# Attention and token mixing on one core: the fourth pair of heads takes f32 weights turned on TensorE, and the fifth pair's scores move ahead of its products

## The chip, the cores and the metric

The kernel runs on one core of a Trainium2 chip. The metric is the device time of one execution in microseconds (us). The engines are named as in the profile: PE is TensorE (PEld its weight loads), DVE is VectorE, ACT is ScalarE, POOL is GpSimd, and SP is the queue from which all DMAs are issued. The granted clock of TensorE stands in the profile as a share of full speed: 1.00 is 2.4 GHz and 0.50 is 1.2 GHz.

## The reference

There are 8 batches, 8 heads, 576 positions and a head dimension of 64. Attention is masked to a window of 128 positions, with a bias that falls with distance; a token-mixing block follows on the concatenated heads.

```python
scores = scale * np.matmul(q, k.transpose(0, 1, 3, 2))
mask = (rel >= 0) & (rel < window)
scores = np.where(mask, scores + bias[None], -1000000000.0)
attn = np.exp(scores - np.max(scores, axis=-1, keepdims=True))
attn = attn / (np.sum(attn, axis=-1, keepdims=True) + 1e-09)
x = np.matmul(attn, v)                      # heads side by side: (8, 576, 512)
theta = x @ w_theta
zr, zi = x * np.cos(theta), x * np.sin(theta)
y = einsum('ts,bsd->btd', w_tok_r, zr) + einsum('ts,bsd->btd', w_tok_i, zi)
u = x + y
out = u + np.maximum(u @ w_ch, 0.0)
```

## The kernel before

The heads are worked in 32 pairs, p0 to p31; four pairs make one batch. For each pair, queries and keys arrive by DMA (`load_pair`), and are split into a high and a low part in fp32r (`split_high`: two ScalarE instructions, writing qh and kh; `split_low`: ql on VectorE, kl on GpSimd). Three products of these parts give the scores. Query positions are cut into five tiles; `SCORES` groups them as tile (0), tiles (1, 2) and tiles (3, 4). `weigh` (line 436) takes the scores from PSUM on VectorE, adds the band and finds the row's least value, and ScalarE applies the exponential (line 439). The weights of a pair lie in two halves in SBUF, called front and back.

Before the weights can multiply the values they must be turned. `flip(half)` does this in one of two ways. A pair with `early` set (the first `PLAIN` pairs) has eight f32 transposes of 128x128 on TensorE into PSUM and one ScalarE copy to pt (line 448); the products are then plain f32 (`ps<-vb,pt`). All other pairs get an f16 high and low half, hl (ScalarE line 453, VectorE line 455), which one DMA transpose turns into pt (line 457); values are split in the same way into vh and vl (lines 369 and 371), and three f16 products are summed. The scale for that split comes from the largest value of each head: a `measure` on VectorE, then `spread_from` and `spread_to`, which use a transpose of `peak` and a small matmul on TensorE.

`values` runs a pair's products over the five tiles and `finish` divides by the sums: denominator (line 486 or 488), reciprocal (491), x_sb (493), all on VectorE. When the four pairs of a batch are in x_sb, `turn` starts: x is transposed on TensorE into columns (L89, `ps<-fixed,x_sb`), split (x_hi at lines 532, 533 and 538; x_lo at 539), multiplied with w_theta (`mm<-wth_hi,x_hi`), and sine and cosine make z. `mix` multiplies z with w_tok, and `channels` makes the output.

The first batch is done by `start`, before anything else overlaps it. Its loop goes over pairs; in round p the pair p-1 has its first half turned, scores of pair p follow, then the second half, more scores, and the products of pair p-1. Between these it unpacks the w_theta and w_tok weights, which arrive as 64-bit floats, in many ScalarE and VectorE passes (lines 169 to 201). In the kernel before, the last round has no new pair: p3 is turned and multiplied alone, and p4's scores are issued after the loop. A scheduler orders the instructions of each engine by its own estimate of time in this part, so instructions of one pair can move ahead of another's; in the order of before, the first tile of p3's scores stands well ahead of the rest. From the first `mix` on, the order on TensorE is pinned to the program's.

PSUM has two rings here: `ps_s`, two tiles of two banks each, for scores of two tiles, turned weights, product sums and columns; and `ps_m`, four banks, for all others. A product sum can start only when the tile two uses earlier in `ps_s` has been read.

Of the kernel before, what the change touches and what calls it, by code (L numbers as in the profile page):

```python
# [20 lines left out]
B, H, S, D = 8, 8, 576, 64  # L21
# [9 lines left out]
DEPTH = 1  # L31
# [2 lines left out]
STEPS, FINISH = ((7, 7, 6, 3), (3, 4, 6, 4), (3, 4, 6, 3)), 250  # L34

GROUP = 4
PLAIN = 3
RINGS = ([("mx", 2 * NT, 4)] + [("den", 2 * NT, 3)] + [("whole", 1, 3), ("vs", GROUP, 3), ("scale", GROUP, 4)]
         + [("whole1", 1, 1), ("vs1", H, 1), ("scale1", H, 1)]
         + [("whole0", 1, 1), ("vs0", 9, 1), ("scale0", 9, 1), ("sum", 9, 1),  # L40
            ("row", 9, 1), ("inv", 9, 1), ("lim", 1, 1), ("t", 1, 2), ("zs", 9, 2), ("back", 1, 2)])
LOWS = float(np.float32(2.0 ** -29 * (1.0 - 2.0 ** -19)))
# [8 lines left out]
def attn_moe_kernel(ctx: ExitStack, tc: tile.TileContext, qt, kt, vx, wth, wtok, wch, band, out):  # L51
# [14 lines left out]
    uf = ctx.enter_context(tc.tile_pool(name="uf", bufs=2))  # L66
    big = ctx.enter_context(tc.tile_pool(name="big", bufs=1))
# [42 lines left out]
    peaks = [const.tile([128, 128], F32, name=f"peak{k}") for k in range(2)]  # L110
# [39 lines left out]
    def unpack(jobs, places):  # L150
# [65 lines left out]
        for k in range(n + 3):  # L216
# [12 lines left out]
    JOBS = ([(wth, wth_hi, wth_lo, c, DM, TURN) for c in range(4)]  # L229
            + [(wtok, wtk_hi, wtk_lo, c, S, "row") for c in ORDER])  # L230
# [18 lines left out]
    group_v = {}  # L249
# [7 lines left out]
    def measure(g, heads):  # L257

        nc.vector.tensor_reduce(out=peaks[g % 2][:, heads], in_=group_v[g][:, heads, :, :64],
                                axis=mybir.AxisListType.XY, op=ALU.max, apply_absolute_value=True)  # L260

    def spread(peak, n, part):
        return spread_to(spread_from(peak, n, part), n, part)
# [28 lines left out]
    def spread_first(g):  # L292
        peak = peaks[g % 2]
        nc.vector.tensor_scalar(out=peak[:, :GROUP], in0=peak[:, :GROUP], scalar1=2.0 ** -100, scalar2=None,
                                op0=ALU.max)
        group_v[g] = group_v[g], spread_from(peak, GROUP, "")

    def spread_scales(g):
        vb, diag = group_v[g]
        scale = spread_to(diag, GROUP, "")  # L300
        group_v[g] = vb, scale
        if g % 2:
            c = rings["scale"].at + (g // 2 - 1) % 2 * 2 * GROUP
            batch_scale(g // 2, fixed[:, c:c + 2 * GROUP])

    whole_w, first_scale = [], []

    def measure_first(g):
        nc.vector.tensor_reduce(out=peaks[0][:, GROUP * g:GROUP * g + GROUP], in_=group_v[g][:, :, :, :64],
                                axis=mybir.AxisListType.XY, op=ALU.max, apply_absolute_value=True)  # L310

    def clamp_first():
        nc.vector.tensor_scalar(out=peaks[0][:, :H], in0=peaks[0][:, :H], scalar1=2.0 ** -100, scalar2=None,
                                op0=ALU.max)
# [14 lines left out]
    def split_pair(p, raw):  # L329
        return split_low(split_high(p, raw))  # L330
# [21 lines left out]
    def split_values(n):  # L352

        k = n % GROUP
        if n < H:
            if k == 0:
                group_v[n // GROUP] = load_plain(n // GROUP)
            vb = group_v[n // GROUP]
            if n < 2 * PLAIN:
                return (vb[:, k],), None, None  # L360
            both = first_scale[0][:, n - n % 2:n - n % 2 + 2]
        else:
            vb, scale = group_v[n // GROUP]
            both = scale[:, k - k % 2:k - k % 2 + 2]
        vs = both[:, n % 2:n % 2 + 1]
        v = vb[:, k, :, :64]
        vh = vp.tile([128, 5, 65], F16, name="vh")
        vl = vp.tile([128, 5, 64], F16, name="vl")
        nc.scalar.activation(vh[:, :, :64], v, AF.Copy, scale=vs)
        nc.gpsimd.memset(vh[:, :, 64:], 1.0)  # L370
        low = nc.vector.scalar_tensor_tensor(out=vl, in0=v, scalar=vs, in1=vh[:, :, :64], op0=ALU.mult,  # L371
                                             op1=ALU.subtract)
        return (vh, vl), both, low
# [7 lines left out]
    SCORES = ((0,), (1, 2), (3, 4))  # L381
# [4 lines left out]
    class Pair:  # L386


        def __init__(self, p):
            self.p = p  # L390
            self.terms = parts.pop(p)
            self.early = p < PLAIN
            self.heads = [Head(2 * p + e, self) for e in range(2)]
# [279 lines left out]
    def prepare(p):  # L673

        if 0 <= p - 1 < pairs and p - 1 not in parts:
            parts[p - 1] = split_pair(p - 1, raw.pop(p - 1))
        if p < pairs and p not in raw:
            raw[p] = load_pair(p)
# [81 lines left out]
    def start(x_sb, load):  # L760

        paces = [0]

        def pace(k=1):
            for _ in range(k):
                paces[0] += 1
                if paces[0] * 2 % 5 < 2:
                    next(load, None)

        next(load)  # L770
        prepare(0)
        nc.sync.dma_start(out=bands, in_=band)
        prepare(1)
        last = None
        for p in range(H // 2 + 1):
            new = Pair(p) if p < H // 2 else None
            if p == 3:
                load_values(2)

            def scores(tiles):  # L780
                if new is not None:
                    new.scores(tiles)
                pace(2 * len(tiles))

            if last is not None:
                last.flip(0)
                scores(SCORES[0])
                scores(SCORES[1])
                last.flip(1)
                scores(SCORES[2])  # L790
                last.values()
                with tc.high_priority(FINISH):
                    last.finish(x_sb)
            else:
                for tiles in SCORES:
                    scores(tiles)
            if new is not None:
                if p == PLAIN:
                    clamp_first()
                    first_scale.append(spread(peaks[0], H, "1"))  # L800
                for head in new.heads:
                    head.ready()
                if p in (1, 2):
                    measure_first(p - 1)
                prepare(p + 2)
            last = new
        for _ in load:
            pass

    first = []  # L810
    st = [dict(b=b) for b in range(B)]
    x_sb = xp.tile([128, NT, DM], F32, name="x_sb")
    start(x_sb, unpack(JOBS, ((big, "u_hi"), (big, "u_lo"), (uf, "xtf"), (uf, "xtf"), (big, "z_hi"), (big, "z_lo"))))
    scales_first()
    for p in range(H // 2, H // 2 + DEPTH):
        measure(p // 2, slice(0, GROUP))
        spread_first(p // 2)
        spread_scales(p // 2)
        first.append(Pair(p))
        for tiles in SCORES:  # L820
            first[-1].scores(tiles)
        for half in range(2):
            first[-1].flip(half)
        prepare(p + 2)
    latest = first[-1].exps
    st[0]["exps"] = latest + copied
    late = unpack(LATE, ((uf, "xtf"),))
# [11 lines left out]
    for b in range(B):  # L839
        chans = channels(b, st[b])  # L840
        mixing = mix(st[b])
        if b + 1 < B:
            x_sb = xp.tile([128, NT, DM], F32, name="x_sb")
# [67 lines left out]
```

## Time and profile before

| What | Value |
|---|---|
| Median of three executions | 668.2 us (667.21 to 669.57) |
| The profiled execution | 667.59 us, its span 665.8 us |
| Busy share of the span | PE 92%, PEld 79%, DVE 79%, ACT 75%, POOL 22% |
| Stage 17 to 34 us | PE 12.67 us busy, DVE 16.03, ACT 17.00, granted clock 0.80 |
| Stage 60 to 70 us | PE 8.47 us busy, DVE 8.56, ACT 7.63, granted clock 0.67 |
| Stage 70 to 80 us | PE 7.37 us busy, DVE 4.92, ACT 2.61, granted clock 0.58 |
| Stage 80 to 90 us | PE 5.79 us busy, DVE 6.48, ACT 9.00, granted clock 0.83 |
| Stage 150 to 550 us | PE 93.8 to 97.4 us busy in each 100 us, granted clock 0.98 to 1.00 |

The busy share is a mean over very different stages. In the first 34 us the DMA engines are busy (shares of 0.92 and 0.97); from 17 to 60 us ScalarE has hardly a free us; from 150 us on TensorE works without pause. A row of a timeline gives the start, the length and the group of instructions, and in brackets how long the engine had been idle before it and what ended the wait. A plain f32 matmul has two records in the trace, so 18 products of one pair count as 36. Lengths of neighbouring TensorE rows overlap slightly, because matmuls are pipelined; starts are the safer numbers.

### The profile page before, as it was taken

The page shows a single profiled execution, that of the slowest core. Times are in us where ns is not written, and L with a number is a line of the kernel's source. Part 1 is how long each engine was busy: PE and PEld are TensorE (multiplying, and loading weights), DVE is VectorE, ACT ScalarE, POOL GpSimd, SP SyncE. Part 2 cuts the span into 40 slices and gives each one's busy share as a digit, 9 for nine tenths or more (in the row PEclk, how much of TensorE's full clock was granted, in tenths as well). Part 3 has the DMA queues.
Part 4 walks back from the last instruction along what each step waited for, and adds up shares of the span by engine and source line. Part 5 has one row for each costly group of instructions (what it writes and reads, how often), then busy time and mean ns, then how long its engine had stood idle before and what let it go on. Part 6 is the DMA issues. An engine that isn't in the chain of part 4 may idle for free.

```text
span 665.8 us, 15029 instructions
## 1 busy us (share of the span) xinstructions
PE 609.4 (92%) x5738; PEld 524.8 (79%) x5738; DVE 525.7 (79%) x1367; ACT 500.0 (75%) x947; POOL 143.2 (22%) x198
## 2 busy tenths in 40 slices
PE   4778689696999999999999999999999999999997
PEld 3767676476888898787887888788878888789887
DVE  5998589898689968997699958997699968965622
ACT  6999499766897869867997679776988789637710
POOL 3010000333022312212122202221212212220220
PEclk9856689798999999999999999999999999999999
DMA  9943630969119860579029940787037810941001
GB/s 268 354 143 108 140 64 14 212 159 192 44 31 215 170 134 28 121 170 223 28 53 196 192 94 26 168 161 196 19 88 177 187 58 24 145 78 46 19 19 54
DMA packets 153256, 80.21 MB, mean 120 GB/s; under 512 B 126304, under 2 KB 142688, under 8 KB 153184
## 3 DMA queue, kind: packets, MB, share of 16 engines
q1 hardware_dynamic: 153184, 79.25, 52.4%
q8 instruction: 45, 0.74, 0.5%
q14 instruction: 27, 0.22, 0.1%
HBM read 39.39 MB, written 9.44 MB: 73 GB/s over the span
## 4 chain that ended last, share of the span: by engine, by line
DVE 30%; PE 29%; ACT 22%; DMA 12%; issue 4%; SPq 1%; POOL 0%; DVEq 0%; ACTq 0%; POOLq 0%
PE mm L74 23%; DMA qr<-in_qt_dram 8%; PE ps L74 5%; DVE hl L455 5%; DMA pt<-hl 4%; DVE front L436 3%; ACT g L567 3%; DVE back L436 2%; ACT g L566 2%; ACT z_hi L515 2%; DVE z_lo L516 2%; DVE g L571 2%; DVE vl L371 2%; ACT front L439 2%; DVE ql L345 2%
## 5 line engine op out<-in xcount | busy, mean ns | idle before, releaser
L74 PE MATMUL mm<-wtk_hi,z_hi 128*128 128x288 f16 x576 | 165.8, 288 | 0.6 <-ACT z_hi L515 0.6
L74 PE MATMUL mm<-wtk_hi,z_lo 128*128 128x288 f16 x576 | 165.1, 287 | 0.5 <-DVE z_lo L516 0.3
L74 PE MATMUL mm<-wtk_lo,z_hi 128*128 128x288 f16 x576 | 165.2, 287 | 0.0
L74 PEld LDWEIGHTS <-z_hi 128*128 128x128 f16 x1152 | 107.6, 99 | 30.7 <-ACT z_hi L515 0.9
L637 POOL TENSOR_TENSOR u_lo<-xtf,u_hi 128x288 fp32r<-128x288 f32 x64 | 51.5, 823 | 172.1 <-DVE vl L371 129.8
L347 POOL TENSOR_TENSOR kl<-kr,kh 128x576 fp32r<-128x576 f32 x31 | 44.7, 1443 | 145.6 <-issue 72.7
L439 ACT ACTIVATE front<-front,fixed 128x256 f32<-128x256 f32 (+2 forms) x160 | 59.6, 444 | 18.3 <-DVE fixed L436 18.2
L74 PEld LDWEIGHTS <-z_lo 128*128 128x128 f16 x576 | 56.5, 98 | 16.2 <-DVE z_lo L516 1.8
L74 PE MATMUL ps<-vh,pt 128*128 128x65 f16 x1044 | 56.9, 199 | 12.4 <-DMA pt<-hl 12.2
L74 PEld LDWEIGHTS <-pt 128*128 128x128 f16 x1566 | 55.1, 101 | 14.6 <-DMA pt<-hl 13.4
L439 ACT ACTIVATE back<-back,fixed 128x256 f32<-128x256 f32 x128 | 56.9, 496 | 0.0
L74 PE MATMUL ps<-vl,pt 128*128 128x64 f16 x522 | 54.6, 197 | 0.0
L338 ACT ACTIVATE qh<-qr 128x640 fp32r<-128x640 f32 x31 | 22.9, 739 | 41.4 <-DMA qr<-in_qt_dram 41.2
L635 ACT CAST u_hi<-xtf 128x288 fp32r<-128x288 f32 x64 | 27.0, 423 | 35.8 <-DVE xtf L633 35.8
L74 PE MATMUL mm<-wth_hi,x_hi 128*128 128x512 f32 x160 | 47.3, 418 | 4.7 <-DVE x_hi L533 4.7
L74 PE MATMUL ps<-kh,qh 64*128 64x256 f32 (+1 forms) x256 | 43.4, 335 | 7.0 <-DVE x_sb L493 6.7
L455 DVE SCALAR_TENSOR_TENSOR hl<-front,hl 128x1024 f16<-128x1024 f32 x29 | 46.6, 1606 | 2.7 <-ACT hl L453 2.5
L436 DVE CUSTOM_DVE_ANT_0 back<-ps,bands 128x256 f32<-128x256 f32 x128 | 46.6, 419 | 0.4 <-PE ps L74 0.4
L74 PE MATMUL mm<-u_hi,wch_hi 128*128 128x288 f32 x256 | 46.6, 304 | 0.0
L633 DVE SCALAR_TENSOR_TENSOR xtf<-mm,fixed,xtf 128x288 f32<-128x288 f32 x64 | 32.0, 508 | 16.9 <-PE mm L74 16.9
L74 PE MATMUL mm<-u_hi,wch_lo 128*128 128x288 f32 x256 | 44.6, 296 | 0.0
L74 PE MATMUL mm<-wth_lo,x_hi 128*128 128x512 f32 x160 | 44.5, 400 | 0.0
(161 smaller groups left out, 1509.0 us busy)
## 6 DMA issues: line engine op xcount, KB each, us to landing
vb<-in_vx_dram SPq DMA_DIRECT2D x16, 650.0 KB, 5.7
out_dram<-xtf SPq DMA_DIRECT2D x64, 144.0 KB, 1.8
kr<-in_kt_dram SPq DMA_DIRECT2D x31, 288.0 KB, 3.6
qr<-in_qt_dram SPq DMA_DIRECT2D x31, 144.0 KB, 3.1
qr<-in_qt_dram SPq DMA_DIRECT2D x31, 128.0 KB, 3.6
xtf<-in_wch_dram SPq DMA_DIRECT2D x4, 512.0 KB, 4.7
z_hi<-in_wtok_dram SPq DMA_DIRECT2D x2, 576.0 KB, 5.8
z_lo<-in_wtok_dram SPq DMA_DIRECT2D x2, 576.0 KB, 6.2
```

Source lines behind the costliest of these rows:

```text
L74: ins = nc.tensor.matmul(*args, **kw)
L338: nc.scalar.activation(qh, qr, AF.Copy, scale=sc)
L345: low = nc.vector.scalar_tensor_tensor(out=ql, in0=qr, scalar=sc, in1=qh.bitcast(F32), op0=ALU.mult, op1=ALU.subtract)
L347: rest = nc.gpsimd.tensor_tensor(out=kl, in0=kr, in1=kh.bitcast(F32), op=ALU.subtract)
L371: low = nc.vector.scalar_tensor_tensor(out=vl, in0=v, scalar=vs, in1=vh[:, :, :64], op0=ALU.mult, op1=ALU.subtract)
L436: self.weighed = nc.vector.tensor_tensor_reduce(out=sb, in0=ps, in1=bias, scale=2.0 ** -(2 * self.p % H + 1), scalar=3.0e38, op0=ALU.add, ...
L439: self.exps.append(nc.scalar.activation(sb, sb, AF.Exp, bias=least, scale=-1.0))
L455: self.lowered = nc.vector.scalar_tensor_tensor(out=hl[:, 1], in0=src, scalar=2.0 ** PEXP, in1=hl[:, 0], op0=ALU.mult, op1=ALU.subtract)
L567: nc.scalar.activation(g[:n], g[:n], AF.Sin, bias=halfpi[:n], scale=-RAD)
L633: nc.vector.scalar_tensor_tensor(out=xtf[:, m, cs], in0=y_ps[:, :HALF], scalar=st["back"], in1=xtf[:, m, cs], op0=ALU.mult, op1=ALU.add)
L635: nc.scalar.copy(u_hi[:, m, cs], xtf[:, m, cs])
L637: return nc.gpsimd.tensor_tensor(out=u_lo[:, m, cs], in0=xtf[:, m, cs], in1=u_hi[:, m, cs].bitcast(F32), op=ALU.subtract)
```

## The change

`PLAIN` becomes 4, so p3 is early too: its weights are turned by 16 f32 transposes on TensorE and copied by ScalarE, and its products are plain f32 matmuls with its unsplit values. The scales for p3's values (`first_scale`, the rings of `whole1`, `vs1`, `scale1`) are gone. The loop of `start` makes a fifth pair, p4, in its last round, so p4's scores stand between p3's turns and products as in the rounds before, and `start` returns p4; the code after the loop keeps p4's peaks and scale and its two flips. Line numbers behind the removed ones shift by up to 11.

```diff
@@ -34,9 +34,8 @@
 STEPS, FINISH = ((7, 7, 6, 3), (3, 4, 6, 4), (3, 4, 6, 3)), 250
 
 GROUP = 4
-PLAIN = 3
+PLAIN = 4
 RINGS = ([("mx", 2 * NT, 4)] + [("den", 2 * NT, 3)] + [("whole", 1, 3), ("vs", GROUP, 3), ("scale", GROUP, 4)]
-         + [("whole1", 1, 1), ("vs1", H, 1), ("scale1", H, 1)]
          + [("whole0", 1, 1), ("vs0", 9, 1), ("scale0", 9, 1), ("sum", 9, 1),
             ("row", 9, 1), ("inv", 9, 1), ("lim", 1, 1), ("t", 1, 2), ("zs", 9, 2), ("back", 1, 2)])
 LOWS = float(np.float32(2.0 ** -29 * (1.0 - 2.0 ** -19)))
@@ -303,7 +302,7 @@
             c = rings["scale"].at + (g // 2 - 1) % 2 * 2 * GROUP
             batch_scale(g // 2, fixed[:, c:c + 2 * GROUP])
 
-    whole_w, first_scale = [], []
+    whole_w = []
 
     def measure_first(g):
         nc.vector.tensor_reduce(out=peaks[0][:, GROUP * g:GROUP * g + GROUP], in_=group_v[g][:, :, :, :64],
@@ -356,12 +355,9 @@
             if k == 0:
                 group_v[n // GROUP] = load_plain(n // GROUP)
             vb = group_v[n // GROUP]
-            if n < 2 * PLAIN:
-                return (vb[:, k],), None, None
-            both = first_scale[0][:, n - n % 2:n - n % 2 + 2]
-        else:
-            vb, scale = group_v[n // GROUP]
-            both = scale[:, k - k % 2:k - k % 2 + 2]
+            return (vb[:, k],), None, None
+        vb, scale = group_v[n // GROUP]
+        both = scale[:, k - k % 2:k - k % 2 + 2]
         vs = both[:, n % 2:n % 2 + 1]
         v = vb[:, k, :, :64]
         vh = vp.tile([128, 5, 65], F16, name="vh")
@@ -773,13 +769,12 @@
         prepare(1)
         last = None
         for p in range(H // 2 + 1):
-            new = Pair(p) if p < H // 2 else None
+            new = Pair(p)
             if p == 3:
                 load_values(2)
 
             def scores(tiles):
-                if new is not None:
-                    new.scores(tiles)
+                new.scores(tiles)
                 pace(2 * len(tiles))
 
             if last is not None:
@@ -794,34 +789,28 @@
             else:
                 for tiles in SCORES:
                     scores(tiles)
-            if new is not None:
-                if p == PLAIN:
-                    clamp_first()
-                    first_scale.append(spread(peaks[0], H, "1"))
+            if p == 3:
+                clamp_first()
+            if p < H // 2:
                 for head in new.heads:
                     head.ready()
-                if p in (1, 2):
-                    measure_first(p - 1)
-                prepare(p + 2)
+            if p in (1, 2):
+                measure_first(p - 1)
+            prepare(p + 2)
             last = new
         for _ in load:
             pass
-
-    first = []
+        return last
+
     st = [dict(b=b) for b in range(B)]
     x_sb = xp.tile([128, NT, DM], F32, name="x_sb")
-    start(x_sb, unpack(JOBS, ((big, "u_hi"), (big, "u_lo"), (uf, "xtf"), (uf, "xtf"), (big, "z_hi"), (big, "z_lo"))))
+    first = [start(x_sb, unpack(JOBS, ((big, "u_hi"), (big, "u_lo"), (uf, "xtf"), (uf, "xtf"), (big, "z_hi"), (big, "z_lo"))))]
     scales_first()
-    for p in range(H // 2, H // 2 + DEPTH):
-        measure(p // 2, slice(0, GROUP))
-        spread_first(p // 2)
-        spread_scales(p // 2)
-        first.append(Pair(p))
-        for tiles in SCORES:
-            first[-1].scores(tiles)
-        for half in range(2):
-            first[-1].flip(half)
-        prepare(p + 2)
+    measure(2, slice(0, GROUP))
+    spread_first(2)
+    spread_scales(2)
+    for half in range(2):
+        first[-1].flip(half)
     latest = first[-1].exps
     st[0]["exps"] = latest + copied
     late = unpack(LATE, ((uf, "xtf"),))
```

TensorE, around p3's turns and products. In the kernel before, p2's products (the first row of `ps<-vb,pt`) are followed by two small matmuls and p3's f16 products, each with its own weight load:

```order
L89 MATMUL mm<-fixed,peak_103 128x128
L74 MATMUL ps<-vb,pt 128x65 x18
L74 MATMUL mm<-fixed 128x9
L89 MATMUL mm<-fixed,peak_103 128x128
L74 LDWEIGHTS pt
L74 MATMUL ps<-vh,pt 128x65
L74 LDWEIGHTS pt
L74 MATMUL ps<-vl,pt 128x64
```

In the kernel after, front_102 and back are p3's halves, and the scores between them are p4's; the last row is the columns of the first batch:

```order
L88 MATMUL mm<-fixed,peak_103 128x128
L73 MATMUL ps<-vb,pt 128x65 x18
L88 MATMUL ps<-fixed,front_102 128x128 x8
L73 MATMUL mm<-fixed 128x9
L88 MATMUL mm<-fixed,peak_103 128x128
...
L88 MATMUL ps<-fixed,back 128x128 x8
L73 MATMUL mm<-fixed 128x4
...
L73 MATMUL ps<-vb,pt 128x65 x18
L88 MATMUL ps<-fixed,x_sb 128x128 x8
```

Two turns of eight transposes have come in, six rows of p4's scores follow each of them, and a second set of 18 plain products stands where the f16 products stood. The f16 products and their weight loads are gone.

ScalarE, at the copy of p2's second turned half (`COPY pt<-ps`). Before, p3's exponentials (front_102) and two scalings of w_tok are ahead of it:

```order
L182 ACTIVATE u_hi,fixed<-u_hi 128x576
L193 ACTIVATE wtk_hi<-z_lo,fixed 128x576
L439 ACTIVATE front_102<-front_102,fixed 128x128 x2
L439 ACTIVATE front_102<-front_102,fixed 128x256 x2
L193 ACTIVATE wtk_hi<-u_hi,fixed 128x576
L448 COPY pt<-ps 128x1024
```

After, with front_101 the first tile of p4:

```order
L181 ACTIVATE u_hi,fixed<-u_hi 128x576
L192 ACTIVATE wtk_hi<-z_lo,fixed 128x576
L435 ACTIVATE front_101<-front_101,fixed 128x192
L435 ACTIVATE front_102<-front_102,fixed 128x128 x2
L444 COPY pt<-ps 128x1024
L435 ACTIVATE front_102<-front_102,fixed 128x256 x2
L192 ACTIVATE wtk_hi<-u_hi,fixed 128x576
```

The copy has moved ahead of two exponentials and one scaling; one exponential of p4 has come in before it. Further down the same queue, p4's value casts, its high halves and p6's key and query splits now all stand between the copy of p3's back half and the first x_hi.

VectorE, from p3's denominators to the first column tile. Before, where front_101 is p4's first half:

```order
L488 SCALAR_TENSOR_TENSOR fixed<-ps,fixed 128x10
L491 RECIPROCAL fixed<-fixed 128x10
L140 TENSOR_SCALAR fixed<-mm 128x4
L493 TENSOR_TENSOR x_sb<-ps,fixed 128x2x5x64
...
L455 SCALAR_TENSOR_TENSOR hl<-front_101,hl 128x1024
L533 TENSOR_TENSOR x_hi<-ps,x_hi 128x4x64
```

After:

```order
L482 TENSOR_SCALAR fixed<-ps 128x10
L451 SCALAR_TENSOR_TENSOR hl<-front_101,hl 128x1024
L487 RECIPROCAL fixed<-fixed 128x10
L489 TENSOR_TENSOR x_sb<-ps,fixed 128x2x5x64
L451 SCALAR_TENSOR_TENSOR hl<-back,hl 128x1024
L529 TENSOR_TENSOR x_hi<-ps,x_hi 128x4x64
```

p4's front low half stands between the denominators and the reciprocal, and its back low half ahead of x_hi; the weighing of p4's scores, which stood between x_sb and the front low half, is now ahead of the denominators.

## Rows read from the trace of the kernel before

**Rows 1.** The chain of waits, 61 to 91 us: start, length, what.

```profile
61.83 1.00 ACT pt L448
...
66.93 5.66 DMA pt<-hl
...
72.64 4.82 PE ps L74 x61
...
81.15 0.56 ACT kh L339
81.71 0.64 ACT qh L338
82.35 0.95 ACT hl L453
...
83.33 1.22 DVE hl L455
...
84.94 5.54 PE mm L74 x16
```

**Rows 2.** The timeline of TensorE: start, length, operation, count, idle time before.

```profile
24.55 5.61 PE L74 MATMUL ps<-vb,pt 128*128 128x65 f32 x36 [0.49 <-ACT pt L448]
...
45.03 7.94 PE L74 MATMUL ps<-vb,pt 128*128 128x65 f32 x36 [2.37 <-DVE fixed L436]
52.77 1.91 PE L89 MATMUL ps<-fixed,front 128*128 128x128 f32 x8
55.75 0.48 PE L74 MATMUL ps<-kh,qh 64*128 64x128 f32 x2 [1.07 <-DVE x_sb L493]
...
57.33 1.97 PE L89 MATMUL ps<-fixed,back 128*128 128x128 f32 x8
59.56 0.58 PE L74 MATMUL ps<-kh,qh 64*128 64x256 f32 x2 [0.26 <-DVE fixed L436]
...
61.15 0.37 PE L89 MATMUL mm<-fixed,peak 128*128 128x128 f32 x1
62.87 6.32 PE L74 MATMUL ps<-vb,pt 128*128 128x65 f32 x36 [1.35 <-ACT pt L448]
68.98 0.54 PE L74 MATMUL mm<-fixed 128*128 128x9 f32 x2
69.37 0.45 PE L89 MATMUL mm<-fixed,peak 128*128 128x128 f32 x1
...
79.41 0.66 PE L89 MATMUL ps<-fixed,x_sb 128*128 128x128 f32 x4
...
84.94 1.90 PE L74 MATMUL mm<-wth_hi,x_hi 128*128 128x512 f32 x4 [3.25 <-DVE x_hi L533]
```

**Rows 3.** Stretches: length, busy PE, PEld, DVE, ACT, POOL; clock; DMA; GB/s.

```profile
50.00:60.00 10.00, 8.67 (x46) 7.67 (x48) 8.31 (x25) 8.94 (x19) 0.01 (x1) 0.50 0.64 180
...
61.00:62.00 1.00, 0.52 (x4) 0.18 (x1) 0.05 (x1) 1.00 (x3) 0.00 (x0) 0.86 0.00 0
...
63.00:64.00 1.00, 1.00 (x10) 1.00 (x11) 1.00 (x7) 1.00 (x2) 0.00 (x0) 1.00 0.00 0
64.00:65.00 1.00, 1.00 (x10) 1.00 (x9) 1.00 (x4) 1.00 (x3) 0.58 (x1) 0.84 0.00 0
...
66.00:67.00 1.00, 1.00 (x6) 1.00 (x7) 1.00 (x3) 0.97 (x3) 0.00 (x0) 0.50 0.26 25
```

**Rows 4.** The timeline of ScalarE, 58 to 81 us.

```profile
58.43 0.68 ACT L182 ACTIVATE u_hi<-u_hi 128x576 f32<-128x576 f32 x1 [1.06 <-DVE fixed L184]
...
59.78 1.48 ACT L439 ACTIVATE front<-front,fixed 128x128 f32<-128x128 f32 x4
...
78.89 1.92 ACT L369 ACTIVATE vh<-vb,fixed 128x320 f16<-128x320 f32 x4 [1.97 <-DVE fixed L142]
```

**Rows 5.** The timeline of VectorE, p3's finish.

```profile
77.50 0.17 DVE L488 SCALAR_TENSOR_TENSOR fixed<-ps,fixed 128x10 f32<-128x10 f32 x1 [1.20 <-PE ps L74]
...
77.95 0.82 DVE L493 TENSOR_TENSOR x_sb<-ps,fixed 128x640 f32<-128x640 f32 x1
```

## The prediction

> **What bounds the kernel now.** I read the page's slices and the table by stage first, then the chain of waits, then the timelines of TensorE, ScalarE and VectorE around the change. From about 150 us on TensorE is busy 94 to 97% and the change touches nothing there; what can move is the prologue, in which the first four pairs of heads are attended and the first batch starts. Below, p0 to p5 are the pairs in order, a "turn" is one half of a pair's weights turned, and "products" are the pair's weights times its values.
>
> The chain through the place of the change [rows 1]: ScalarE copies the second half of p2's turned weights at 61.83 us, TensorE runs p2's products from 62.87 [rows 2], a DMA transpose that turns p3's weights is issued at 66.93 and lands 5.66 us later, p3's products (with half of p4's scores between them) start at 72.64, then ScalarE casts values and splits key and query and makes p4's high half (82.35), VectorE makes the low half (83.33), and only then is the first column tile split, whose products with w_theta start at 84.94. I call this last moment T. From the eight x_sb transposes on, all instructions stand in the same order on every engine in both kernels, so the time is won or lost by how T moves, as far as DMA and clock behind T stay alike.
>
> **What the clock does here.** It comes first, since the change puts TensorE work on this stretch. p0's products took 5.61 us, p1's 7.94, p2's 6.32 [rows 2], 36 records each. The granted clock tells why [rows 3]: 1.00 (2.4 GHz) from 63 to 64 us, with ten records in that us, and 0.50 (1.2 GHz) from 66 to 67, with six. By the shares 0.86 and 0.84 it rose at about 61.3 and fell at about 64.7. Before it rose, scores, a turn and scores had stood nearly without a gap from 55.75 to 61.5; it fell while the products ran. In p1's products and the turn behind them at 52.77 [rows 2], TensorE had no gap for 9.7 us, and their length is that of half clock. So f32 products do not earn the full clock here and lose it; scores and turns side by side earned it.
>
> The Trainium skill (TensorE: Matmul & The Clock Gate, Part 1) says that a TensorE that is kept busy is given its full clock. The trace of p1's products differs, and the measurement decides. The Trainium skill (the same page, Part 4, PE-mode transpose) says that transposes do not count as busy in the same way; by that the new turns would not lift the clock. The trace leans against it, since a turn of 1.97 us was part of the stretch before the rise.
>
> **The change part by part, in the order of time.**
>
> Removed at 35 to 49 us: the spread of the peaks of p0 to p3 (two small matmuls, a few VectorE rows) and the split of p3's values (two ScalarE casts, two VectorE rows). ScalarE is full there, so about 1.0 comes free by the row of four casts, 1.92 [rows 4]; but the next thing TensorE waits for, p1's products, already runs, and VectorE still waits for w_tok words. I cost it at nothing by itself; between -1.0 by those casts and +0.3, a third of a scores row, for p4's first tile that now stands ahead of p3's scores, in a gap that TensorE has before 55.75.
>
> Start of p2's products, 62.87 before. The copy of the second turned half started 2.5 us after its turn (57.33 + 1.97 = 59.30 [rows 2], 61.83 [rows 1]): ahead of it on ScalarE stood an absolute-value pass that waited 1.06 for VectorE, a w_tok scaling, exponentials of 1.48 [rows 4] and another scaling. In the new order it stands ahead of half of the exponentials and of the last scaling, so it can end at about 60.4. TensorE's own queue has p3's last scores (59.56 to 61.15) and a small transpose before the products [rows 2], done by 61.5 at half clock and earlier at full. I take 60.9: -2.0 (bounds -1.4 and -2.5).
>
> p2's products: 3.6 us by ten records in a us, 7.94 at half clock throughout. Before, they came after 1.35 us of idling [rows 2]; now turn, tile, scores, turn and scores stand with hardly a gap from 53 us on, and they start at the full clock more surely. The nearest row is p0's 5.61, which also began at full; between it and 3.6 I take 5.0: -1.3. They end at 65.9 (69.2 before).
>
> Then the new block on TensorE. At half clock: front turn 1.91; the 9-wide matmul and the peak transpose 0.85 (68.98 to 69.82); p4's first scores 1.6, like the last ones; back turn 1.97; the 4-wide matmul 0.5; p4's last scores 1.6; sum 8.4 [rows 2]. Its waits are covered: x_sb of p2 is there 1.3 us after the products [rows 5], the copy of the front turn (1.0 [rows 1]) lies under p4's first scores, the weighing on VectorE under the back turn. At the full clock the sum is 4.2, but a copy and the weighing then show, some 5.3. The block is longer than the stretch that lifted the clock before, so I let the clock rise about halfway: 6.8. p3's products start at 72.7.
>
> p3's products were 54 f16 matmuls and are now f32 like the first three: 3.6 to 7.94, by the same choice 5.0; they end at 77.7 (77.5 before). Gone are the wait for the DMA, two low halves of 1.2 on VectorE and the small splits; ScalarE has two copies of 1.0 in place of two casts of 1.0.
>
> From the end of p3's products to T, 7.5 us before: the casts, key and query and p4's high half held the column tile back. Now they stand earlier on ScalarE, beside p3's products; but VectorE has p4's front low half between p3's denominators and the reciprocal. So: denominator, reciprocal and x_sb 1.3 [rows 5], low half 1.2 [rows 1], eight x_sb transposes 1.9 at half clock (four took 0.66 at full [rows 2]); the back low half and both parts of x_hi lie beside these. Sum 4.4 (3.5 at full). ScalarE sets a floor: after the copy of the back turn it has two exponentials 0.7, four casts 1.9, key and query 1.2, a high half 0.95, four exponentials 1.5 and a high half 0.95 [rows 1, 4], in all 7.2 before x_hi. With the copy done at about 72.2 that is 79.4, below the 81 to which x_hi comes; it binds if the block runs at the full clock. T is 77.7 + 4.4 = 82.1 against 84.94.
>
> An added wait: on SP the load of a later value group must wait until p3's products have read its buffer, and p4's two DMA transposes are queued behind it. They need the low halves that VectorE makes after those same products, so they lose nothing, and p4's products come only after the whole z work. Cost 0; at most 0.5, should the 0.65 MB land beside the transposes. Behind T the first four w_theta products took 1.90 [rows 2] at half clock, so there is little to lose; if the clock rises later there, up to +1.
>
> **The sum.** Start of p2's products -2.0, their length -1.3, then 6.8 + 5.0 + 4.4 = 16.2 where 84.94 - 69.19 = 15.75 stood: -2.8. The profiled execution took 667.59 us (span 665.8 and 1.8 around it), so the forecast is 664.8. The median of the three runs shown, 668.2, is 0.6 above the profiled one, within their spread of 2.4.
>
> **Rivals.**
>
> 1. Slower: the turns do not lift the clock, and it stays at 0.50 as it did from 50 to 60 us [rows 3]. p2's products start at 61.4 and take 6.32, the block 8.4, p3's products 7.94, the tail 4.4: T = 88.5, +3.5, 671.1. It decides for the slower side once both products take more than 13 us together with the block at half clock. For it: every product row spent much of its length at half clock. Against it: the rise at 61.3.
>
> 2. No change: the clock rises only for the first part of the products, as for p0; both take 5.61 and the block stays at 8.4. T = 61.4 + 5.6 + 8.4 + 5.6 + 4.4 = 85.4, +0.5, 668.1. What the DMA wait gave is eaten by 16 f32 transposes and 36 f32 records.
>
> 3. Much faster: the full clock all along, since TensorE has no gap. p2's products 60.4 to 64.0, block 5.3, p3's 3.6 to 72.9; ScalarE's floor then binds: copy done at 69.2, x_hi at 76.4, T about 77.3: -7.6, 660.0. Against it: p1's products. It is where Part 1 of the page above, in the Trainium skill, would lead.
>
> **How the numbers follow.** Forecast 0.45, rival 1 0.17, rival 2 0.28, rival 3 0.10. The forecast alone has 662.5 to 666.6, by products of 3.6 to 5.6. The range for 8 in 10 cuts part of rivals 1 and 3: 661.0 to 670.0. A change under 0.3% (2.0 us) cannot be told from none. Faster than 666.2 holds rival 3 and nearly all of the forecast, 0.54; rival 2 and the forecast's rest are within, 0.29; slower 0.17.
>
> **What would show it.** In the profile after: p2's products starting near 61 and not 62.9; a granted clock of 1.00 at their start and again when p3's products start; p3's products of 4 to 5.6 us; hardly any idle time before them; x_hi waiting for the transposes and not for ScalarE; T near 82; and from T on the same distance to the end. Wrong would be: a clock of 0.50 from 65 to 80 us (rival 1), ScalarE's queue ending the wait before the w_theta products (towards rival 3), or a T that moves while the end stays, which would mean that something behind T takes up the gain.

## The result and the profile after

The kernel after takes 659.05 us (median of four runs, 657.60 to 660.76) against 668.16 (667.21 to 669.57): a ratio of 0.9863, 95% interval 0.9833 to 0.9892, or 9.1 us faster by the medians. The forecast was 664.8 and the range 661 to 670, so the time lies below the range. The profiled execution took 657.60 us with a span of 655.8; against the one of before it is 10.0 us shorter. Of that, T (the start of the first w_theta products) gives 6.15 us: 78.79 against 84.94 [rows 2]. The other 3.85 come behind T, where both kernels have the same instructions; how much of these 3.85 belongs to one execution only, the second runs below show.

TensorE's timeline after, the rows that answer to [rows 2] (start, length, operation, count, idle time before):

```profile
45.36 7.94 PE L73 MATMUL ps<-vb,pt 128*128 128x65 f32 x36 [3.02 <-ACT pt L444]
53.09 1.91 PE L88 MATMUL ps<-fixed,front 128*128 128x128 f32 x8
54.66 0.51 PE L73 MATMUL mm<-kh,qh 128*128 128x192 f32 x1
...
56.46 1.09 PE L88 MATMUL ps<-fixed,back 128*128 128x128 f32 x8
58.33 0.39 PE L73 MATMUL ps<-kh,qh 64*128 64x256 f32 x2 [0.77 <-DVE fixed L432]
...
60.24 4.23 PE L73 MATMUL ps<-vb,pt 128*128 128x65 f32 x36 [0.52 <-ACT pt L444]
64.31 1.04 PE L88 MATMUL ps<-fixed,front 128*128 128x128 f32 x8
...
66.60 0.33 PE L73 MATMUL ps<-kh,qh 64*128 64x128 f32 x2 [0.94 <-DVE fixed L139]
...
67.48 1.09 PE L88 MATMUL ps<-fixed,back 128*128 128x128 f32 x8
...
69.92 4.23 PE L73 MATMUL ps<-vb,pt 128*128 128x65 f32 x36
...
76.83 1.33 PE L88 MATMUL ps<-fixed,x_sb 128*128 128x128 f32 x5 [2.34 <-DVE x_sb L489]
78.79 2.08 PE L73 MATMUL mm<-wth_hi,x_hi 128*128 128x512 f32 x4 [0.62 <-DVE x_hi L529]
```

p2's products take 4.23 us instead of 6.32, p3's 4.23 as well, and every turn behind 55 us 1.04 to 1.09 instead of 1.9. The row at 54.66 is p4's first score tile: it stands where TensorE idled 1.07 us before (the wait at 55.75 in [rows 2] is gone). The windows that answer to [rows 3] (stretch, length, busy PE, PEld, DVE, ACT, POOL; clock; DMA; GB/s) show why the rows are short:

```profile
50.00:60.00 10.00, 8.76 (x60) 7.86 (x59) 8.92 (x30) 9.21 (x19) 0.00 (x0) 0.74 0.57 175
61.00:62.00 1.00, 1.00 (x12) 1.00 (x10) 1.00 (x2) 1.00 (x2) 0.00 (x0) 1.00 0.00 0
...
64.00:70.00 6.00, 4.74 (x51) 4.22 (x49) 5.07 (x26) 3.37 (x7) 0.00 (x0) 1.00 0.36 100
70.00:75.00 5.00, 4.49 (x39) 4.25 (x39) 2.07 (x10) 5.00 (x11) 0.00 (x0) 1.00 0.02 3
75.00:76.00 1.00, 0.00 (x0) 0.00 (x0) 0.96 (x3) 1.00 (x3) 0.00 (x0) 0.85 0.62 65
76.00:82.00 6.00, 4.54 (x13) 3.46 (x14) 4.46 (x7) 3.91 (x7) 0.00 (x0) 0.50 1.05 275
```

By its share of 0.74 over the first stretch the clock rose at about 55.2. It stayed at 1.00 through both product sets and the whole block, and fell at about 75.7 (0.85), when TensorE had been without work for 1.2 us. What ended last before T is another chain than [rows 1] (start, length, what):

```profile
70.40 1.91 ACT vh L365 x4
72.31 0.56 ACT kh L338
72.87 0.64 ACT qh L337
73.51 0.95 ACT hl L449
74.46 1.60 ACT back L435 x4
76.08 1.07 ACT hl L449
77.17 1.23 DVE hl L451
78.40 0.35 DVE x_hi L529
78.79 5.69 PE mm L73 x16
```

No DMA is in it. ScalarE works without a gap from the copy of p3's back half (68.70 to 69.69) to p4's second high half, and VectorE's low half then holds x_hi back. On VectorE (the rows that answer to [rows 5]) p4's front low half stands between denominator and reciprocal, as the order said:

```profile
74.20 0.17 DVE L482 TENSOR_SCALAR fixed<-ps 128x10 f32<-128x10 f32 x1 [2.69 <-PE ps L73]
74.57 1.23 DVE L451 SCALAR_TENSOR_TENSOR hl<-front,hl 128x1024 f16<-128x1024 f32 x1 [0.20 <-ACT hl L449]
75.71 0.21 DVE L487 RECIPROCAL fixed<-fixed 128x10 f32<-128x10 f32 x1
75.95 0.82 DVE L489 TENSOR_TENSOR x_sb<-ps,fixed 128x640 f32<-128x640 f32 x1
```

Behind T, the page's table of DMA issues (count, median us from issue to landing) differs in a row that the change doesn't touch, the 56 transposes of the later pairs. Before:

```profile
pt<-hl SPq DMA_TRANSPOSE x58, 5.1
```

After:

```profile
pt<-hl SPq DMA_TRANSPOSE x56, 4.6
```

With it goes a wait of ScalarE from 150 to 560 us (us in all, times, the longest), for loads that are queued on SP behind the transposes. Before:

```profile
ACT qh L338 <- DMA qr<-in_qt_dram: 36.6, 18, 3.7
```

After:

```profile
ACT qh L337 <- DMA qr<-in_qt_dram: 21.9, 15, 2.7
```

### The profile page after: what moved, and what is told of

Same layout as the page of the kernel before. It is cut to its first block, busy times and chain, and to the rows that moved or that the text cites. A ratio compares the mean times of both kernels' runs of the same rounds, so it can differ in the third digit from the quotient of the medians.

```text
span 655.8 us, 14992 instructions
## 1 busy us (share of the span) xinstructions
PE 607.6 (93%) x5733; PEld 524.0 (80%) x5733; DVE 524.3 (80%) x1359; ACT 500.6 (76%) x945; POOL 143.5 (22%) x196
## 4 chain that ended last, share of the span: by engine, by line
PE 41%; DVE 27%; ACT 20%; DMA 7%; issue 3%; SPq 0%; POOL 0%; DVEq 0%; ACTq 0%; POOLq 0%
PE mm L73 33%; PE ps L73 7%; DVE hl L451 5%; DMA qr<-in_qt_dram 4%; ACT g L563 3%; DVE front L432 2%; ACT z_hi L511 2%; ACT g L562 2%; DMA pt<-hl 2%; DVE g L567 2%; DVE z_lo L512 2%; ACT front L435 2%; DVE xtf L629 2%; DVE f L567 2%; PE ps L88 2%
## 5 line engine op out<-in xcount | busy, mean ns | idle before, releaser
L435 ACT ACTIVATE front<-front,fixed 128x128 f32<-128x128 f32 (+2 forms) x160 | 60.3, 444 | 14.3 <-DVE fixed L432 14.0
L73 PE MATMUL ps<-vh,pt 128*128 128x65 f16 x1008 | 52.9, 197 | 8.8 <-DMA pt<-hl 8.8
L73 PEld LDWEIGHTS <-pt 128*128 128x128 f16 x1512 | 51.9, 100 | 10.0 <-DMA pt<-hl 9.1
L73 PE MATMUL ps<-vl,pt 128*128 128x64 f16 x504 | 51.0, 195 | 0.0
L661 DVE SCALAR_TENSOR_TENSOR xtf<-mm,xtf 128x288 f32<-128x288 f32 x64 | 29.0, 454 | 20.8 <-PE mm L73 20.7
```

The source lines that it names most:

```text
L73: ins = nc.tensor.matmul(*args, **kw)
L435: self.exps.append(nc.scalar.activation(sb, sb, AF.Exp, bias=least, scale=-1.0))
L661: nc.vector.scalar_tensor_tensor(out=xtf[:, e, cs], in0=o_ps[:, :HALF], scalar=0.0, in1=xtf[:, e, cs], op0=ALU.max, op1=ALU.add)
```

## The experiments

Two questions: what moved T, and what moved the distance behind it. To take the clock of the z stage out of the second, I read from each profile also Z, the start of the first w_tok product (94.96 after, 100.95 before), and the distance from Z to the span's end: 560.84 after, 564.85 before. The stretch from T to Z is called the z stage.

**Both kernels again** (one run each).

> The kernel before, a second profile. Between the two profiles shown, 6.15 us were gained before T (the start of the w_theta products) and 3.8 us behind it, where no instruction was changed. Theory 1 (chance of an execution behind T): T again near 84.9, but the distance from T to the end of the span differs from 580.9 by 1 us or more. Theory 2 (the kernel before always loses there): that distance again within 0.5 us of 580.9.

> The kernel after, a second profile. Theory 1 (chance behind T): the distance from T to the end differs from 577.0 by 1 us or more, T again near 78.8. Theory 2 (the new kernel always gains there): it is within 0.5 us of 577.0. If the clock before T depends on the execution, T lies 2 us or more from 78.8, with p2's and p3's products longer than 4.23 us.

Before took 669.35 us with T 85.79, after 661.51 with T 79.24: T moved by 6.55, though here the clock rose only at 61.2 in the kernel after, and at 91.2 in the one before. The gain in T is not an accident of one profile. The distance from T to the end is less steady: 581.71 before (0.85 from the first profile, between the two theories) and 580.46 after, 3.45 from the first profile, as theory 1 has it; a third profile of the kernel after (g4) has T 79.18 and 577.12. From Z the three of the kernel after have 560.84, 563.33 and 560.87. So the distance of a single profile says little here, and what follows rests on medians of several runs and on groups of profiles.

**e1: the turns alone.** p3 is turned on TensorE, but p4's scores come after the loop.

```diff
-            new = Pair(p)
+            new = Pair(p) if p < H // 2 else None
...
+    first.append(Pair(4))
+    for tiles in SCORES:
+        first[-1].scores(tiles)
```

> The kernel after, but p4's scores issued after the loop as in the kernel before: the f32 turns alone. Theory A (the gain is the full clock, which p4's first tile in TensorE's gap near 55 us and its scores between the turns keep up): the gap is open again, p2's products take about 6 us, p3's 5 to 8, T 83 to 87, the time 666 to 670. Theory B (the gain is the DMA wait that went): the time is within 2 us of the kernel after, 657 to 661.

665.06 us, ratio 0.9941 (0.9920 to 0.9963); T 85.35. TensorE's rows:

```profile
61.74 7.94 PE L73 MATMUL ps<-vb,pt 128*128 128x65 f32 x36
...
74.28 4.15 PE L73 MATMUL ps<-vb,pt 128*128 128x65 f32 x36
...
85.35 2.07 PE L73 MATMUL mm<-wth_hi,x_hi 128*128 128x512 f32 x4 [2.27 <-DVE x_hi L529]
```

p2's products ran at half clock (it rose at 74.1). T is where theory A had it, and the time a little below its 666. Without p4's scores the removed DMA wait gives T nothing, so the 3.9 us (by the ratio) come from behind T. Their size is that of an address alone, as f2 below shows (0.9945).

**e2: the scores alone.** The kernel before, with p4 in the last round and p3 still turned by DMA.

```diff
-            new = Pair(p) if p < H // 2 else None
+            new = Pair(p)
...
```

> The kernel before with p4's scores moved into the last round, p3 still turned by DMA: the moved scores alone. Theory A: the first tile fills the gap near 55 us, the clock rises there, p2's products take 4 to 5 us and end near 65, T comes to 79 to 81 although p3 still waits for its DMA; the time is 661 to 664. Theory B: the wait for the DMA stays, so T is 83 to 85 and the time 666 to 669.

672.19 us, ratio 1.0059 (1.0027 to 1.0091): slower by 0.6%, above the range of either theory. The profiled execution, 668.13, is the fastest of seven, so it doesn't show where the others lost their time; that stays open. In its profile p2's products have the full clock,

```profile
60.11 4.23 PE L74 MATMUL ps<-vb,pt 128*128 128x65 f32 x36
...
73.69 0.23 PE L74 MATMUL ps<-vh,pt 128*128 128x65 f16 x1 [2.06 <-DMA pt<-hl]
```

but p3's products still wait for the DMA and start later than before (72.64); T is 82.99, at the edge of theory B's 83 to 85 and 2.0 to 2.8 earlier than in the two profiles of the kernel before. So the scores bring the clock and the turns remove the wait that swallows most of it; the 6 us of T need both.

**e5: p4's first tile late.** The kernel after with that tile behind p3's front turn.

```diff
...
                 last.flip(0)
-                scores(SCORES[0])
+                with tc.issue_after(last.turned.ins) if p == 4 else nullcontext():
+                    scores(SCORES[0])
```

> The kernel after with p4's first score tile (three matmuls of 128x192) held behind p3's front turn on TensorE; in the kernel after it fills the gap before 55.7 us. The estimate of the scheduler shifts a few ScalarE and VectorE rows with it. Theory A: the clock is lifted by turns and scores that stand without a gap from 53 us on, so with the gap back the clock rises later, p2's products take 5 to 8 us instead of 4.2, and T is 81 to 83. Theory B: the tile does nothing for the clock (in a second profile of the kernel after it rose only at 61.2 and T was 79.2 all the same); then p2's products take 4.2, and T is 79 to 80.

665.2 us in one run, p2's products 7.94 us; the clock rose at 73.1. T is 84.72:

```profile
84.72 2.08 PE L73 MATMUL mm<-wth_hi,x_hi 128*128 128x512 f32 x4 [1.98 <-DVE x_hi L530]
```

Theory A, and by more than it said. Over all profiles: where the tile fills the gap ahead of 56 us, p2's products took 4.1 to 4.5 us in 11 of 12; where it doesn't (before twice, e1, e4, e5, f2), 6.3 to 8.0 in 6 of 6. How the tile brings the clock is not shown: among the twelve it rose between 54.8 and 62.5 us, at times only when p2's products had begun.

**e3 and e4: small DMAs.** Each DMA on SP takes the next of eight completion semaphores, and two DMAs less shift all later ones.

```diff
+    small = const.tile([128, 8], F32, name="small")
...
+    for c in range(0, 8, 4):
+        nc.sync.dma_start(out=small[:, c:c + 4], in_=x_sb[:, 0, 448:452])
```

> The kernel after with two small DMAs added (4 columns of x_sb into an unused tile, 2 KB each), issued on SP beside p4's two DMA transposes; every other row on every engine stands as in the kernel after. SP's DMAs take eight completion semaphores in turn, so from there on every DMA has the semaphore that it had in the kernel before. Theory A: the part of the gain that appears behind T (3.9 us between the two shown profiles) hangs on which of the eight slots the later DMA transposes and loads take; then T stays at 79 and the distance from T to the end goes back to 581 or more, time 661 to 663. Theory B: the slots don't matter, and the distance differs because two DMA transposes less in the prologue leave the later stages in another phase; then T is 79, the distance 577 to 580.5 as in the two profiles of the kernel after, time 658 to 661. Median landing of the DMA transposes 5.0 to 5.1 us by A, 4.6 by B.

> The kernel before with six small DMAs of the same kind ahead of p4's two DMA transposes on SP; all other rows stand as in the kernel before. Six more is two less by count of eight, so from there on every DMA has the semaphore that it has in the kernel after. Theory A (the slots): T stays at 85 to 86, or up to 1 later if the six delay p4's DMA transposes, and the distance to the end falls to 577 to 580, time 664 to 666; the DMA transposes land in 4.6 us at the median. Theory B (not the slots): distance 581 to 582, time 667 to 669, 5.0 to 5.1 us.

e3: 663.01 us, T 79.22, T to the end 581.38, landing 5.1: as theory A said. e4: 670.01 us, T 85.73, distance 580.77, landing 5.2: as theory B said. So the slots are not the cause. What e3, e4 and before share against after and e1 is something that I had not thought of: each has a tile more in the constants (`small`, or the rings that the change removed), so hl and pt lie at other SBUF addresses. In the kernel after they start on a multiple of 512 bytes, before 96 above one, in e3 32, in e4 192.

**f1 to f4: addresses alone.** Only an unused tile is added (96, 416, 128 and 256 bytes a partition); the order of all instructions stays.

```diff
     scratch = const.tile([128, 1], F32, name="scratch")
+    pad = const.tile([128, 24], F32, name="pad")
```

> The kernel after with an unused tile of 96 bytes a partition behind the constants, and nothing else: every row on every engine stands as in the kernel after, but the tiles behind it (hl and pt among them) have the SBUF addresses that they have in the kernel before (96 above a multiple of 512 bytes; in the kernel after they lie on one, since the removed rings made the constants shorter). Theory A: the DMA transposes from hl to pt are quicker where the tiles lie on a multiple of 512 bytes, and this is the gain behind T; then T is 79, the distance to the end 581 to 582, the transposes land in 5.0 to 5.2 us at the median, time 662 to 664. Theory B (two DMA transposes less put the later stages in another phase, addresses are nothing): distance 577 to 580.5, landing 4.6, time 658 to 661.

> The kernel before with an unused tile of 416 bytes a partition behind the constants, and nothing else: hl and pt now lie on a multiple of 512 bytes as in the kernel after; all rows stand as in the kernel before. Theory A (addresses): T stays at 85 to 86, the distance to the end falls to 577 to 579, landing 4.6, time 664 to 666. Theory B (not the addresses): distance 581 to 582, landing 5.1, time 667 to 669.

> The kernel after with an unused tile of 128 bytes: hl and pt lie 128 above a multiple of 512. If theory A holds and 512 counts: landing 5.0 to 5.2, distance 581 or more. If a multiple of 128 is enough: 4.6, and 577 to 580.5. The kernel with six small loads, at 192 above, had 5.2, so a multiple of 64 isn't.

> The kernel after with an unused tile of 256 bytes: hl and pt lie 256 above a multiple of 512. If theory A holds and 512 counts: landing 5.0 to 5.2, distance 581 or more. If a multiple of 256 is enough: 4.6, and 577 to 580.5.

f1, after with the addresses of before: 661.47 us, ratio to before 0.9914 (0.9886 to 0.9942), T 79.59, distance 581.41: theory A, with the time half a us below its 662.

```profile
pt<-hl SPq DMA_TRANSPOSE x56, 5.3
```

f2, before with addresses like those of after: 665.09 us, ratio 0.9945 (0.9924 to 0.9967).

```profile
pt<-hl SPq DMA_TRANSPOSE x58, 4.7
```

An unused tile makes the kernel before 3.7 us faster by the ratio (2.2 to 5.1). f3 (660.65 us in one run, distance 580.40 where 581 or more was expected) landed in 5.1; f4, at 256 (662.79 us in one run), in

```profile
pt<-hl SPq DMA_TRANSPOSE x56, 4.6
```

so a multiple of 256 bytes is enough and 128 is not. The two ratios multiply to 0.9859, the 0.9863 of the whole change. In f2's profile, which at 666.22 us is one of the two slowest of its ten executions, the distance from T did not fall as foretold (580.94): the clock was at half from 82.4 to 89.7, and T to Z took 17.10 us against 16.01 before; from Z the distance is 563.84. Nor did T stay at 85 to 86: it is 83.46. SP's row for p3's two transposes is 3.81 us long there and 5.81 in the kernel before, and p3's products start at 71.07, right behind p2's, with no wait for the DMA. So a part of the wait that the change removes came from the address too. No run has p4's scores in the last round, p3 turned by DMA and hl on a multiple of 256; how much of T the turns would still give there is open.

f4 showed something else as well: T 83.06. The clock fell at 63.6, during p2's products, and stayed low through the block:

```profile
64.00:73.00 9.00, 9.00 (x49) 8.55 (x48) 6.26 (x25) 3.26 (x8) 0.89 (x4) 0.50 0.24 66
```

It is the one in 12 above. What decides it is open.

**g1 and g2: source or destination.** g1 moves pt, and the tiles behind it, by 96 bytes, and leaves hl. g2 moves hl, and the tiles ahead of it, by 96 and pt by 256. g1's edit:

```diff
+    gap = ctx.enter_context(tc.tile_pool(name="gap", bufs=1))
     ptp = ctx.enter_context(tc.tile_pool(name="ptp", bufs=4))
...
+    gap.tile([128, 24], F32, name="pad")
```

> The kernel after with 96 unused bytes a partition between hl's and pt's tiles: hl, the source of the DMA transposes, stays on a multiple of 512 bytes, pt, the destination, lies 96 above one. If the destination counts, the transposes land in 5.0 to 5.3 us at the median; if only the source counts, in 4.5 to 4.7.

> The kernel after with 96 unused bytes ahead of hl's tiles and 160 between hl's and pt's: hl lies 96 above a multiple of 256, pt on a multiple of 256. If the destination alone counts, 4.5 to 4.7 us; if the source counts, 5.0 to 5.3; if each costs a part, between.

g1, pt moved (658.98 us):

```profile
pt<-hl SPq DMA_TRANSPOSE x56, 4.8
```

g2, hl moved (660.22 us):

```profile
pt<-hl SPq DMA_TRANSPOSE x56, 5.3
```

Of the two it is the source that counts. g1's 4.8 is a little above the 4.5 to 4.7 expected, but g3 below, with pt unmoved, has 4.8 as well. One rival remains: each run that moves hl off its place also moves the tiles that the loads of queries, keys and values fill, and slower loads could hold up the transposes. The DMA packets in the traces speak against it. The packets of 256 bytes, nearly all of them the transposes', took 21.8 to 23.0 ns at the mean where hl lies on a multiple of 256 and 24.3 to 25.5 elsewhere, and 19.0 to 19.5 against 20.5 to 21.2 while no larger packet was under way. The packets of the value loads (1300 bytes) took 69.5 to 74.1 ns in the first group and 67.8 to 70.5 in the second, so the loads are not the slower ones. All eighteen profiles by the place of hl:

| hl above a multiple of 256 bytes | Kernels | Landing, us | Z to the end, us |
|---|---|---|---|
| 0 | after (3 profiles), e1, e5, e6, g3, f2, f4, g1 | 4.5 to 4.8 | 560.8 to 564.0, mean 562.3 |
| 32, 96, 128 or 192 | before (2), e2, e3, e4, f1, f3, g2 | 5.0 to 5.3 | 563.6 to 566.9, mean 564.7 |

The landings don't overlap; the distances do a little, with means of 562.27 and 564.72, 2.45 us apart. That is no more than the three profiles of the kernel after differ among themselves, so the size of the gain rests on f1's and f2's medians.

**e6 and g3: p4's splits held back**, since they end the wait for T in the kernel after.

```diff
-    for half in range(2):
-        first[-1].flip(half)
...
+            while halves:
+                with behind_all([st[0]["split"], st[0]["kept"]]):
+                    first[-1].flip(halves.pop(0))
```

> The kernel after with p4's two f16 splits (hl, ScalarE 1.0 each and VectorE 1.2 each) and their DMA transposes held behind the first column tile's split; TensorE and SP keep their order. Theory: ScalarE's queue (copy, exponentials, four casts, key and query, two high halves) and VectorE's two low halves end the wait before T in the kernel after. Without the halves x_sb comes 1.2 earlier (VectorE: 75.6 instead of 76.8), ScalarE is free at 75.2, x_hi at about 77.0, T 77.2 to 77.7 instead of 78.8: -1.1 to -1.6, time 657 to 658, if the distance to the end stays. Rival: the halves then stand in the z stage, between x_hi and the first sine, and cost there what they gave: T 77.5, distance +1 to +1.5, time within 0.5 of the kernel after.

> The kernel with p4's splits held behind the first column tile, a second time, on one chip with the kernel after. By its first profile T is 77.5 against 78.8 to 79.6, so 1 to 2 us faster than g4 where the distance to the end stays; no difference if the splits cost in the z stage what they give.

> The kernel after once more: 658 to 661 us, T 78.5 to 79.6 with the clock up through both product sets; T near 83 if the clock falls in p2's products as in f4.

T came to 77.51 and 77.29, as expected, and the clock stayed up through the z stage, so Z is 92.20 and 91.99: about 3 us ahead of the kernel after. But in the profiles the lead is lost again, in two steps. By a late w_tok product of the same batch it is 1.08. TensorE waits there for z: in e6 0.30 and 0.48 us for z_lo from VectorE at 96.58 and 100.05, waits that the kernel after doesn't have. The halves that were held back now stand in that stage; that they are the reason is argued and not shown. After:

```profile
103.38 0.30 PE L73 MATMUL mm<-wtk_hi,z_hi 128*128 128x288 f16 x1 [0.62 <-ACT z_hi L511]
```

e6:

```profile
102.30 0.30 PE L73 MATMUL mm<-wtk_hi,z_hi 128*128 128x288 f16 x1 [0.62 <-ACT z_hi L511]
```

In the next batch p5's first f16 product waits for its DMA in both. After:

```profile
122.79 0.24 PE L73 MATMUL ps<-vh,pt 128*128 128x65 f16 x1 [4.04 <-DMA pt<-hl]
```

e6:

```profile
122.78 0.23 PE L73 MATMUL ps<-vh,pt 128*128 128x65 f16 x1 [5.11 <-DMA pt<-hl]
```

There nothing is left of it (0.45 us between g3 and g4), and the distance from T to the end is 578.59 and 578.71 against 577.01 and 577.12: near what the rival said. The medians lie further apart than the profiles: 658.25 (ratio 0.9839, 0.9811 to 0.9868), and on one chip 657.46 (0.9828, 0.9796 to 0.9860) against 660.01 for the kernel after (0.9864, 0.9833 to 0.9894). By these g3 is 2.5 us faster, with four runs of each and intervals that overlap, so whether holding the splits back gains anything is open.

## Why the prediction was wrong

The direction and the mechanism in T were right; the miss of 7.2 us in the profiled execution (664.8 against 657.60) is 3.3 in T and 3.9 behind it. The terms, forecast and measured:

| Term | Forecast, us | Measured, us |
|---|---|---|
| p2's products start | 60.9 | 60.24 |
| their length | 5.0 | 4.23 |
| the block of turns and scores | 6.8 | 5.45 |
| p3's products | 5.0 | 4.23 |
| from their end to T | 4.4 | 4.64 |
| T | 82.1 | 78.79 |
| T to the span's end | 580.86 (as before) | 577.01 |

- **The clock, mis-sized.** The step that failed is "I let the clock rise about halfway: 6.8", with the 5.0 for each product set. I read from the rows of before that f32 products lose the full clock; in 11 of 12 profiles with the tile in the gap p2's products run at it, and in the profile after the block took 5.45 and each set 4.23. Behind it stands an edit that I "cost at nothing by itself": p4's first tile in the gap. By e5, one profile in which a few other rows moved too, T is 84.7 without it, 5.5 to 5.9 later than in the three profiles of the kernel after: the largest single piece of T. The 3.6 us that I took for the full clock, from ten records in a us, was too low as well: a set takes 4.1 to 4.5, and the kernel after has twelve records in the us from 61 to 62 with a set of 4.23, so the count in one us is not the pace of the set.
- **The waits.** The copy did end earlier, and p2's products started 2.6 earlier than before, where I had 2.0. In the block only 0.94 and 0.32 us of waiting show, close to the 1.1 between my 4.2 and 5.3 for the full clock.
- **ScalarE's floor was right** in size: 7.2 from the copy's end to x_hi by rival 3, 7.7 measured (69.69 to 77.35). That rival, with a chance of 0.10, was the way it went, at 660.0; its T of 77.3 left out VectorE's low halves; with both engines' halves held back, e6 has 77.51, 1.3 earlier. That its 660.0 lies near the median of 659.05 is in part luck: T came 1.5 us later than it said, and the gain behind T was in no rival.
- **"From T on the same distance to the end" failed.** The condition "as far as DMA and clock behind T stay alike" hid a term. The removed rings (17 columns) moved hl by 96 bytes, onto a multiple of 256. I had costed the removed values' scale by its instructions and not by its bytes. f1, where the addresses stay, took 661.5, inside the range, still 3.3 below the forecast.
- Rivals 1 and 2 did not come, though f4, with T 83.06, is what a clock that falls in the products looks like.

## What to carry to other kernels

When a diff changes the size of a tile, list where the tiles behind it land, above all the sources of DMA transposes: the same instructions ran 3.7 us faster with an unused tile in front (f2). A small piece of TensorE work in a gap can be worth more than its length where the gap decides the clock of the stage behind it, so read the clock of that stage and not only the wait. And where a chain has a second engine just under the first, as ScalarE and VectorE here, the next wait is already there: moving T forward by another 1.3 us (e6) had left no lead in the profile by p5's products, since z, and then a DMA of the next batch, kept TensorE waiting.

## What the runs showed of the hardware

- **DMA transposes of the same size (2 x 1024 f16 a partition) landed in 4.5 to 4.8 us where their source starts on a multiple of 256 bytes, and in 5.0 to 5.3 elsewhere;** moving the destination alone left them within the first range (4.8 in g1). The Trainium skill (DMA: Bandwidth & Descriptors, "How a descriptor splits into AXI transactions") says that a read starts on a multiple of 256 bytes, and that one which begins between two also fetches the bytes ahead of it. By that rule a source that is off costs more, and the trace agrees: 5.3 us in g2, with the source 96 bytes off and the destination on a multiple of 256. That page does not speak of transposes there, and no run here shows the descriptors.
- **The 36 records of a set of f32 products took 4.23 us at 1.00 and 7.94 at 0.50.** In the kernel after they kept the full clock through two sets, and idle times of 0.94 and 0.32 us between 64 and 70 us did not bring it down; it fell at 75.7, 1.2 us after TensorE ran out of work. The products can lose it all the same: in the kernel before and in f4 it fell inside p2's set (64.7 and 63.6), and in before_again, e3, e5, f3 and f4 within 1.2 us of the start of p1's set, behind 2.4 to 3.1 us of idling.
